# Attention and a cosine MLP on one core: global score products in tiles of 64 columns, and global value products two slots earlier

## The chip, the cores and the metric

The kernel runs on one core of a Trainium2 chip. The metric is the device time of one execution in microseconds (us). The kernel before takes 924.01 us, the median of three runs (923.69 to 924.47). Its profiled execution, from which all rows below are read, took 926.0 us with a span of 924.2 us.

A core has five engines that run side by side, each through its own list of instructions and in the order of that list: PE (TensorE, the matmuls; its weight loads are the extra line PEld), DVE (VectorE), ACT (ScalarE), POOL (GpSimd) and SP (SyncE, which starts most DMAs). They wait for each other only by semaphores. Matmuls write to PSUM, from which ACT and DVE read.

## The reference

```python
def _attn_ref(q_l, k_l, v_l, q_g, k_g, v_g):     # 8 batches, 8 heads, 512 local + 32 global rows, head size 64
    k_all = np.concatenate([k_g, k_l], axis=2)
    v_all = np.concatenate([v_g, v_l], axis=2)
    s_g = scale * np.matmul(q_g, k_all.transpose(0, 1, 3, 2))     # global rows see all 544 keys
    out_g = np.matmul(sm(s_g), v_all)
    ...                                           # s_ll: local rows see |i - j| <= 32, s_lg: and the 32 global keys
    out_l = np.matmul(sm(np.concatenate([s_lg, s_ll], axis=-1)), np.concatenate([v_g, v_l], axis=2))
    return np.concatenate([out_g, out_l], axis=2)

def _moe_ref(x, w_in, w_out):                     # x: 4608 x 512, w_in: 512 x 2048, w_out: 2048 x 512
    h = x @ w_in
    return ((h * np.cos(h)) @ w_out).astype(np.float32)
```

The rows of the attention's output, with the heads side by side, are the rows of `x`.

## The kernel before, in words

Every float32 number that goes into a product is split into a high and a low float16 part (names that end in h and l), and a product is the sum of three terms: high by high, low by high, high by low. For batches 0 to 2 the score products still run in float32.

**Attention.** A batch is cut into four units: two halves of the heads' groups by two halves of the rows. A unit multiplies queries and keys (`ps`, L574), takes the exponential (`t`, ACT), writes two planes of weights (`planes`), has them transposed by a DMA (`pt`, L704), and multiplies them with the values (`acc`, L746). ACT and DVE then split `acc` into `xh` (L769) and `xl` (L770), the inputs of the MLP. The global rows are a small side line of the same stages: scores `gps` (L789 in float32, L798 in float16) of four heads, minimum (`gt`, L811), exponential, planes `planes_g`, a transposing DMA to `ptg` (L839), value products `gacc` (L851), and a sum of these into `xg` on DVE (L866, L867), which is needed only for the last chunk of the MLP.

**MLP.** Chunks of 256 rows: `ph` = x by w_in (L923), eight of them in a chunk (`ph_0` to `ph_7`); ACT makes an integer of it (`u`, L946), DVE the rest (L947), ACT the cosine (`w`, L461), DVE the product (`gf`, L966), ACT its high part (`gh`, L970), POOL its low part (`gl`, L253), and PE multiplies with w_out (`po`, L996). `o` is the output on its way to memory.

**Order.** Work is put into slots: `at(slot, phase, f)` notes that the step f belongs to a slot and a phase of that slot. A unit has four slots, and its steps are placed relative to its own slot t: the scores of the global rows at `t + s_gs1`, the value products of the unit (`av_a`) at `t`, phase PA, the global value products (`g_f`) and their sum (`g_g`) at `t + s_gf`. From ranks made of slot and phase a list scheduler, which simulates the engines, writes the order of every engine's list. So a moved step also changes the order of steps that the diff does not touch.

**Buffers.** `gps`, `gacc`, `acc` and `ps` share PSUM tiles of the tag att (three buffers), `ph` has three, `po` two. `ptg` has one buffer.

**Start.** In the first 160 us the weights are still being split: `wo_hl` is written piece by piece (POOL, L253), and the first chunk's `po` products and some column sums of them (`po<-wo_hl,xh`) follow as the pieces come.

Of the kernel before, what the change touches and what calls it, by code (L numbers as in the profile page):

```python
# [23 lines left out]
SG = 32  # L24
# [80 lines left out]
FB = 3  # L105
# [10 lines left out]
s_gs1 = -4  # L116
s_gd = -3
s_ge = -1
s_gf = 2
s_v = -12  # L120
s_va = -8
W0 = -15
# [30 lines left out]
def body(tc, qf, v, wi, wo, mask, out):  # L153
    nc = tc.nc
    from contextlib import ExitStack

    with ExitStack() as ctx:
# [297 lines left out]
        st = {}  # L455
# [324 lines left out]
        def g_a(b, g, k):  # L780
            z, w = GW[k]
            pt = ps.tile([P, w], F32, tag="att", name=f"gps_{b}_{g}_{k}")

            for hh in range(4):
                if b >= FB:
                    break
                q, k_ = st["qk", b, k, 2 * g + hh // 2]
                c = hh % 2 * SG
                nc.tensor.matmul(  # L789
                    pt[32 * hh : 32 * hh + 32], q[:, c : c + SG], k_[:, z : z + w], start=True,  # L790
                    stop=True, tile_position=(0, 32 * hh), skip_group_check=True,
                )
            if b >= FB:
                for n, (x, y) in enumerate(((0, 2), (0, 3), (1, 2))):
                    for hh in range(4):
                        qk = st["qk", b, k, 2 * g + hh // 2]
                        c = hh % 2 * SG
                        nc.tensor.matmul(  # L798
                            pt[32 * hh : 32 * hh + 32], qk[x][:, c : c + SG], qk[y][:, z : z + w], start=n == 0,
                            stop=n == 2, tile_position=(0, 32 * hh), skip_group_check=True,  # L800
                        )
            st["gps", b, g, k] = pt

        def g_b(b, g, k):
# [230 lines left out]
        def at(slot, phase, f, *a, pr=None):  # L1035
            e = (phase, len(ev[slot]), f, a)
            ev[slot].append(e)
            pr = (slot, phase) if pr is None else pr if isinstance(pr, tuple) else (pr, phase)
            rank[slot, e[1]] = pr + (slot, e[1])
# [3 lines left out]
        def attn(b, h, g, o):  # L1043
            first = (b, h, g) < (0, 1, 0)
            if b or h and not EL:
                at(o["load"], PJ, load_qk, b, h, g)
            if b >= FB:
                at(o["load"] + s_qm - s_load, PG, q_m, b, h, g)
                at(o["host"], PC, q_s, b, h, g)
                at(max(o["host"], o["load"] + s_qh - s_load), PF, q_h, b, h, g)  # L1050
            for a in range(2):
                p = 2 * g + a
                at(o["sc"][a], PA, sc_a, b, h, p)
                for i in (2 * h, 2 * h + 1):
                    at(o["sc"][a], PA if first else PC, sc_b, b, p, i)
                    at(o["ex"][a], PI, sc_c, b, p, i)
                    at(o["sd"][a], PF, sc_d, b, p, i)
                    at(o["tr"][a], PA2, sc_e, b, p, i)
                if h == 0:
                    at(o["vd"][a], PF2, v_d, b, p, *((0,) if b == 0 else ()))  # L1060
                elif b == 0:
                    at(o["vd"][a], PF2, v_d, b, p, 1)
                at(o["av"][a], PA, av_a, b, h, p)
                at(-6 if first else o["av"][a], PF, av_b, b, h, p)
            at(o["gs"], PA, g_a, b, g, h)
            at(o["gs"], PA if first else PC, g_b, b, g, h)
            if h:
                at(o["ex"][1], PI, g_c, b, g)
                at(o["gd"], PF2, g_d, b, g)
                at(o["ge"], PA2, g_e, b, g)  # L1070
                at(o["gf"], PG, g_f, b, g)
                at(o["gf"], PH2, g_g, b, g)

        def steady(t):
# [23 lines left out]
        for g in range(2):  # L1098
            attn(0, 0, g, tight(U0 + 2 * g))
# [21 lines left out]
        for n in range(2, 4 * B):  # L1121
            b, h, g = n // 4, n // 2 % 2, n % 2
            t = 4 * n + T0 - EARLY.get(n, 0)
            if n % 4 == 0:
                at(t + s_v, PA0, load_v, b)
                at(t + s_va, PF, v_a, b)
                at(t + s_va, PG, v_b, b)
                at(t + s_va, PG2, v_c, b)
            attn(b, h, g, steady(t))
# [116 lines left out]
```

## Time and profile before

| what | value |
|---|---|
| median of three runs | 924.01 us |
| profiled execution, span | 926.0 us, 924.2 us |
| PE busy | 875.5 us, 95% of the span |
| ACT busy | 715.5 us, 77% |
| DVE busy | 635.9 us, 69% |
| POOL busy | 336.4 us, 36% |
| chain that ended last | PE 59%, ACT 17%, DVE 14% |

PE is busy nearly all the time, but its ends are modelled: a PE that waits a few tenths of a microsecond still reads as busy. Whether PE or ACT and DVE set the pace of a stretch is told by who waits for whom there. A row of a timeline gives the start, the duration, the engine, the line, the operation, output and inputs by their names, and in brackets how long the engine stood idle before it and who released it.

### The profile page before, as it was taken

The page shows a single profiled execution, that of the slowest core. Times are in us where ns is not written, and L with a number is a line of the kernel's source. Part 1 is how long each engine was busy: PE and PEld are TensorE (multiplying, and loading weights), DVE is VectorE, ACT ScalarE, POOL GpSimd, SP SyncE. Part 2 cuts the span into 40 slices and gives each one's busy share as a digit, 9 for nine tenths or more (in the row PEclk, how much of TensorE's full clock was granted, in tenths as well). Part 3 has the DMA queues.
Part 4 walks back from the last instruction along what each step waited for, and adds up shares of the span by engine and source line. Part 5 has one row for each costly group of instructions (what it writes and reads, how often), then busy time and mean ns, then how long its engine had stood idle before and what let it go on. Part 6 is the DMA issues. An engine that isn't in the chain of part 4 may idle for free.

```text
span 924.2 us, 21213 instructions
## 1 busy us (share of the span) xinstructions
PE 875.5 (95%) x8055; PEld 589.3 (64%) x8055; DVE 635.9 (69%) x1737; ACT 715.5 (77%) x1472; POOL 336.4 (36%) x690
## 2 busy tenths in 40 slices
PE   5568898999999999999999999999999999999998
PEld 3445564566666666666666666666666666666676
DVE  5997886367665967787768876796778766654221
ACT  6869987578777878888788878897888878865443
POOL 6838766233223222233223322332232322333232
PEclk9586998999999999999999999999999999999999
DMA  9949563344534435334534454444533332430000
GB/s 371 417 182 252 125 178 133 79 93 91 135 97 93 103 80 138 73 98 91 156 77 90 85 123 110 103 98 81 145 73 85 60 70 47 84 61 23 1 25 23
DMA packets 163943, 102.79 MB, mean 111 GB/s; under 512 B 149504, under 2 KB 149888, under 8 KB 161792
## 3 DMA queue, kind: packets, MB, share of 16 engines
q1 hardware_dynamic: 163840, 101.43, 43.7%
q8 instruction: 63, 1.03, 0.5%
q14 instruction: 40, 0.33, 0.1%
HBM read 55.79 MB, written 8.91 MB: 70 GB/s over the span
## 4 chain that ended last, share of the span: by engine, by line
PE 59%; ACT 17%; DVE 14%; issue 4%; POOL 3%; DMA 2%; SPq 0%; DVEq 0%; ACTq 0%; POOLq 0%
PE po L996 26%; PE ph L923 25%; ACT t L461 4%; PE ps L574 3%; ACT L461 3%; ACT w L461 3%; DVE u L947 2%; PE acc L746 2%; ACT planes L683 2%; DVE t L627 2%; DVE qkr L609 2%; ACT u L946 2%; ACT qh L608 1%; DMA raw_wi<-wi 1%; POOL wi_l L253 1%
## 5 line engine op out<-in xcount | busy, mean ns | idle before, releaser
L253 POOL TENSOR_TENSOR gl<-gf,gh 128x128 f16<-128x128 f32 x528 | 222.3, 452 | 443.5 <-ACT gh L970 423.6
L996 PE MATMUL po<-wo_hl,gh 128*128 128x512 f16 (+1 forms) x1088 | 314.3, 374 | 4.2 <-POOL wo_hl L253 4.1
L923 PE MATMUL ph<-xl,wi_h 128*128 128x256 f16 x1024 | 279.9, 274 | 1.7 <-DVE xl L770 1.7
L923 PE MATMUL ph<-xh,wi_h 128*128 128x256 f16 x1024 | 279.9, 275 | 0.6
L923 PE MATMUL ph<-xh,wi_l 128*128 128x256 f16 x1024 | 279.1, 274 | 0.0
L923 PEld LDWEIGHTS <-wi_h 128*128 128x128 f16 x2176 | 206.9, 98 | 48.3 <-issue 14.1
L996 PE MATMUL po<-wo_hl,gl 128*128 128x512 f16 (+1 forms) x544 | 199.8, 374 | 0.0
L996 PEld LDWEIGHTS <-gh 128*128 128x128 f16 x1088 | 106.6, 98 | 96.4 <-issue 1.6
L966 DVE SCALAR_TENSOR_TENSOR gf<-w,ph 128x512 f32<-128x512 f32 x136 | 93.3, 686 | 107.2 <-ACT w L461 107.0
L461 ACT ACTIVATE w<-u,pvs_hp,cs 128x512 f32<-128x512 f32 x136 | 110.3, 813 | 58.2 <-DVE u L947 56.5
L947 DVE SCALAR_TENSOR_TENSOR u<-u,cs,ph 128x512 f32<-128x512 int32 x136 | 101.3, 745 | 64.7 <-ACT u L946 64.6
L946 ACT ACTIVATE u<-ph,pvs_hp,cs 128x512 int32<-128x512 f32 x136 | 104.3, 768 | 28.5 <-PE ph L923 28.5
L461 ACT ACTIVATE t<-t,mn 128x192 f32<-128x192 f32 (+1 forms) x256 | 116.6, 458 | 6.1 <-DVE mn L627 5.8
L923 PEld LDWEIGHTS <-wi_l 128*128 128x128 f16 x1088 | 107.0, 98 | 18.1 <-issue 4.6
L970 ACT CAST gh<-gf 128x512 f16<-128x512 f32 x132 | 80.5, 610 | 38.5 <-DVE gf L966 30.3
L683 ACT ACTIVATE planes<-t,sm 128x224 f16<-128x224 f32 (+1 forms) x244 | 91.0, 453 | 5.2 <-DVE sm L650 5.2
L996 PEld LDWEIGHTS <-gl 128*128 128x128 f16 x544 | 53.4, 98 | 64.6 <-issue 5.3
L684 DVE SCALAR_TENSOR_TENSOR planes<-t,sm,planes 128x224 f16<-128x224 f32 (+1 forms) x244 | 92.4, 442 | 0.0
L461 ACT ACT_TABLE_LOAD x60 | 77.0, 1283 | 1.8 <-PEq L1236 0.7
L627 DVE CUSTOM_DVE_ANT_0 t<-ps,msk,qs 128x192 f32<-128x192 f32 (+1 forms) x160 | 59.7, 429 | 0.0
L769 ACT ACTIVATE xh<-acc,xs 128x256 f16<-128x256 f32 x64 | 29.4, 465 | 33.1 <-DVE xl L770 24.5
L746 PE MATMUL acc<-pt,vh 128*64 128x128 f16 (+2 forms) x896 | 45.8, 229 | 7.2 <-ACT pt L702 3.4
(187 smaller groups left out, 1099.3 us busy)
## 6 DMA issues: line engine op xcount, KB each, us to landing
qkr<-qf SPq DMA_DIRECT2D x32, 672.0 KB, 4.0
vr<-v SPq DMA_DIRECT2D x8, 1280.0 KB, 6.7
out<-o SPq DMA_DIRECT2D x33, 256.0 KB, 2.5
raw_wm<-wo SPq DMA_DIRECT2D x10, 512.0 KB, 11.3
raw_wi<-wi SPq DMA_DIRECT2D x4, 1024.0 KB, 16.8
wo_hl<-wi SPq DMA_DIRECT2D x4, 1024.0 KB, 19.0
raw_wo<-wo SPq DMA_DIRECT2D x8, 512.0 KB, 4.6
wi_h<-wo SPq DMA_DIRECT2D x4, 512.0 KB, 7.4
```

Of the source, the lines that this page charges most:

```text
L253: nc.gpsimd.tensor_tensor(o[..., c], a[..., c], b[..., c], op=op)
L461: ins = nc.scalar.activation(*a, **k).ins
L627: st["mn"] = nc.vector.tensor_tensor_reduce(t[:, h], pt[h], msk[:, MOFF[i] : MOFF[i] + w], nal, 3.0e38, ALU.add, ALU.min, mn[:, h : h + 1] ...
L683: a = nc.scalar.activation(hi, t[:, h], AF.Identity, scale=r)
L684: d = nc.vector.scalar_tensor_tensor(lo, t[:, h], r, hi, op0=ALU.mult, op1=ALU.subtract)
L746: mm = nc.tensor.matmul(acc[64 * h : 64 * h + 64, q_out : q_out + n0 * len(segs)], vt[:, tl, 64 * h : 64 * h + 64], rhs, start=(k == 0 and ...
L923: nc.tensor.matmul(ph[:, a], w[:, t // 8, kc, f], x[:, kc, q], start=first and ip == 0, stop=last and ip == 2, skip_group_check=True,)
L946: nc.scalar.activation(k, ph, AF.Identity, scale=st["cs", c][4], bias=quarter)
L947: nc.vector.scalar_tensor_tensor(u, k, m, ph, op0=ALU.mult, op1=ALU.subtract)
L966: nc.vector.scalar_tensor_tensor(gf, w, -0.5, st.pop(("ph", c, j)).rearrange("p a b -> p (a b)"), op0=ALU.mult, op1=ALU.mult,)
L970: nc.scalar.copy(gh, gf)
L996: mm = nc.tensor.matmul(po[n], g[:, a * CT + k * P : a * CT + (k + 1) * P], w[:, 2 * j + a, c0:c1], start=(j == 0 and i == 0), stop=(j == ...
```

## The change

Two things. First, a score tile `gps` holds four heads of 32 rows each. Before, each head has a matmul of its own, in a tile of 32 columns; now two heads that lie side by side in the same operand go in one matmul of 64 columns. There are two matmuls for a term in place of four. Second, `g_f` and `g_g` move from slot t+2 to slot t, and `g_f` from phase PG to phase PA2, behind the unit's own value products.

```diff
-s_gf = 2
+s_gf = 0
...
-            for hh in range(4):
-                if b >= FB:
-                    break
-                q, k_ = st["qk", b, k, 2 * g + hh // 2]
-                c = hh % 2 * SG
-                nc.tensor.matmul(
-                    pt[32 * hh : 32 * hh + 32], q[:, c : c + SG], k_[:, z : z + w], start=True,
-                    stop=True, tile_position=(0, 32 * hh), skip_group_check=True,
-                )
-            if b >= FB:
-                for n, (x, y) in enumerate(((0, 2), (0, 3), (1, 2))):
-                    for hh in range(4):
-                        qk = st["qk", b, k, 2 * g + hh // 2]
-                        c = hh % 2 * SG
-                        nc.tensor.matmul(
-                            pt[32 * hh : 32 * hh + 32], qk[x][:, c : c + SG], qk[y][:, z : z + w], start=n == 0,
-                            stop=n == 2, tile_position=(0, 32 * hh), skip_group_check=True,
-                        )
+            terms = ((0, 1),) if b < FB else ((0, 2), (0, 3), (1, 2))
+            for n, (x, y) in enumerate(terms):
+                for a in range(2):
+                    qk = st["qk", b, k, 2 * g + a]
+                    nc.tensor.matmul(
+                        pt[64 * a : 64 * a + 64], qk[x][:, : 2 * SG], qk[y][:, z : z + w], start=n == 0,
+                        stop=n == len(terms) - 1, skip_group_check=True,
+                    )
...
-                at(o["gf"], PG, g_f, b, g)
+                at(o["gf"], PA2, g_f, b, g)
                 at(o["gf"], PH2, g_g, b, g)
```

PE, at the end of batch 3's last local value products (`acc_1_2`; `gps_0_0` is a score tile of batch 4, `ph_0` the first product of the next chunk), before. A number behind the last underscore only tells tiles of a name apart:

```order
L746 MATMUL acc_1_2_6040<-pt_3_2_5959,vl_3_4809 64x128
L798 LDWEIGHTS qh_0_0_5561
L798 MATMUL gps_0_0_6077<-qh_0_0_5561 32x288
...
L798 MATMUL gps_0_0_6077<-qh_0_0_5561,qkr_0_0_5180 32x288
L923 LDWEIGHTS wi_h
L923 MATMUL ph_0_6116<-xh_4934,wi_h 128x256
```

The same place now:

```order
L746 MATMUL acc_1_2_5992<-pt_3_2_5911,vl_3_4779 64x128
L788 LDWEIGHTS qh_0_0_5519
L788 MATMUL gps_0_0_6029<-qh_0_0_5519 64x288
...
L788 MATMUL gps_0_0_6029<-qh_0_0_5519,qkr_0_0_5144 64x288
L841 LDWEIGHTS vh_2_4774
L841 MATMUL gacc_1_6036<-ptg_1_5914,vh_2_4774 64x2x32
...
L841 MATMUL gacc_1_6036<-ptg_1_5914,vl_3_4779 64x32
L913 LDWEIGHTS wi_h
L913 MATMUL ph_0_6105<-xh_4898,wi_h 128x256
```

The scores have half the matmuls, each of 64 columns as those of `acc` before them, and the 40 matmuls of `gacc`, which stood behind a later unit's `ps`, follow directly.

DVE at the same place, where it splits the two `acc` tiles, before:

```order
L609 SCALAR_TENSOR_TENSOR qkr_0_1_5564<-qkr_0_1_5564,qs_0_1_5971,qh_0_1_5976 128x1344
L770 SCALAR_TENSOR_TENSOR xl_4935<-acc_1_2_6040,xs,xh_4934 128x256
L811 ISA gt_0_6090,gmn_0_6091<-gps_0_0_6077,zero,qs_0_0_5556 128x288
L811 ISA gmn_0_6091 128x1
L770 SCALAR_TENSOR_TENSOR xl_4935<-acc_1_2_6040,xs,xh_4934 128x256
L966 SCALAR_TENSOR_TENSOR gf_7_6109<-w_7_6025,ph_7_5999 128x512
```

And now:

```order
L609 SCALAR_TENSOR_TENSOR qkr_0_1_5522<-qkr_0_1_5522,qs_0_1_5923,qh_0_1_5928 128x1344
L801 ISA gt_0_6077,gmn_0_6078<-gps_0_0_6029,zero,qs_0_0_5514 128x288
L801 ISA gmn_0_6078 128x1
L770 SCALAR_TENSOR_TENSOR xl_4899<-acc_1_2_5992,xs,xh_4898 128x256
L856 TENSOR_REDUCE xg<-gacc_1_6036 128x64
L549 SCALAR_TENSOR_TENSOR vl_3_6335<-vr_5197,vs_5675,vh_3_6334 128x640
L857 TENSOR_SCALAR xg<-xg,pvs_hp 128x64
L770 SCALAR_TENSOR_TENSOR xl_4899<-acc_1_2_5992,xs,xh_4898 128x256
L956 SCALAR_TENSOR_TENSOR gf_7_6098<-w_7_5977,ph_7_5951 128x512
```

The minimum `gt` now stands ahead of both `xl`, and `xg` with the value split `vl_3` of the next batch between them; before, these three stood some 13 us later.

PE in the start phase, first row of each stretch, before: `acc_0_0` is the first value product of batch 1, `po_0<-wo_hl,xh` waits for a piece of the weights:

```order
L746 MATMUL acc_0_0_1918<-pt_0_0_1728,vh_0_1433 64x128
...
L996 MATMUL po_0_1138<-wo_hl,xh_682 128x512
...
L746 MATMUL acc_0_0_1918<-pt_0_0_1728,vl_0_1434 64x128
...
L923 MATMUL ph_4_1998<-xh_680,wi_h 128x256
...
L923 MATMUL ph_5_2067<-xh_680,wi_h 128x256
...
L996 MATMUL po_0_1138<-wo_hl,xh_682 128x512
```

And now:

```order
L913 MATMUL ph_3_1865<-xh_676,wi_h 128x256
...
L746 MATMUL acc_0_0_1908<-pt_1_0_1833,vh_1_1429 64x64
...
L913 MATMUL ph_4_1986<-xh_676,wi_h 128x256
...
L913 MATMUL ph_5_2055<-xh_676,wi_h 128x256
...
L986 MATMUL po_0_1132<-wo_hl,xh_678 128x512
...
L913 MATMUL ph_5_2055<-xl_677,wi_h 128x256
```

All of `acc_0_0` (32 matmuls more), all of `ph_4` (24) and 7 of `ph_5` now stand ahead of the `po` group that stood behind the first 16 matmuls of `acc_0_0`.

## Rows read from the trace of the kernel before

**Rows 1.** Busy us (count) of PE, PEld, DVE, ACT, POOL in windows; PE clock, DMA
```profile
160.00:300.00 140.00, 139.95 (x1219) 91.67 (x1220) 85.24 (x245) 104.34 (x223) 42.97 (x95) 1.00 0.46 99
400.00:500.00 100.00, 99.51 (x979) 66.77 (x978) 76.62 (x210) 83.62 (x175) 29.66 (x67) 1.00 0.43 101
```

**Rows 2.** Waits from 160 to 300 us: total us, times, longest
```profile
ACT u L946 <- PE ph L923: 7.4, 6, 4.1
```

**Rows 3.** Waits from 300 to 800 us
```profile
ACT w L461 <- DVE u L947: 30.9, 35, 2.1
ACT xh L769 <- DVE xl L770: 21.5, 14, 1.7
...
PE ph L923 <- DVE xl L770: 1.7, 5, 0.4
```

**Rows 4.** Chain of waits, 440 to 492 us: start, us, what
```profile
443.46 0.76 PE gacc L851 x40
444.27 0.77 ACT u L946
...
487.73 2.56 PE ph L923 x22
```

**Rows 5.** Waits from 820 us to the end
```profile
ACT u L946 <- PE ph L923: 17.8, 14, 2.3
```

**Rows 6.** Timeline of PE around a score tile
```profile
332.28 0.28 PE L746 MATMUL acc<-pt,vh 128*64 128x128 f16 x4
332.39 0.22 PE L746 MATMUL acc<-pt,vl 128*64 128x128 f16 x2
332.54 0.31 PE L798 MATMUL gps<-qh 128*32 128x288 f16 x4
332.67 0.30 PE L798 MATMUL gps<-qkr,qh 128*32 128x288 f16 x4
```

**Rows 7.** Timeline of PE around the global value products
```profile
417.83 0.26 PE L574 MATMUL ps<-qkr,qh 64*128 64x224 f16 x2
417.92 0.26 PE L574 MATMUL ps<-qh,qkr 64*128 64x224 f16 x2
418.11 0.22 PE L851 MATMUL gacc<-ptg,vh 128*64 128x64 f16 x2
```

**Rows 8.** Timeline of SP: the transposing DMA of the global planes
```profile
421.50 1.30 SPq L839 DMA_TRANSPOSE ptg<-planes_g  x1
```

**Rows 9.** Timeline of DVE where two value tiles are split
```profile
435.96 0.51 DVE L811 CUSTOM_DVE_ANT_0 gt<-gps,zero,qs 128x288 f32<-128x288 f32 x1
436.58 0.48 DVE L770 SCALAR_TENSOR_TENSOR xl<-acc,xs,xh 128x256 f16<-128x256 f32 x1
438.79 0.69 DVE L966 SCALAR_TENSOR_TENSOR gf<-w,ph 128x512 f32<-128x512 f32 x1 [1.72 <-ACT w L461]
```

**Rows 10.** Timeline of ACT at that place
```profile
436.08 0.47 ACT L769 ACTIVATE xh<-acc,xs 128x256 f16<-128x256 f32 x1 [1.72 <-DVE xl L770]
```

**Rows 11.** Timeline of DVE at the old place of the sum
```profile
448.80 0.28 DVE L866 TENSOR_REDUCE xg<-gacc 128x64 f32<-128x128 f32 x1
449.00 1.07 DVE L549 SCALAR_TENSOR_TENSOR vl<-vr,vs,vh 128x640 f16<-128x640 f32 x1
449.99 0.41 DVE L867 TENSOR_SCALAR xg<-xg,pvs_hp 128x64 f32<-128x64 f32 x1
```

**Rows 12.** Timeline of ACT: two places where `w` waits for DVE
```profile
425.66 0.81 ACT L461 ACTIVATE w<-u,pvs_hp,cs 128x512 f32<-128x512 f32 x1 [1.53 <-DVE u L947]
...
451.10 0.81 ACT L461 ACTIVATE w<-u,pvs_hp,cs 128x512 f32<-128x512 f32 x1 [1.01 <-DVE u L947]
```

**Rows 13.** Start phase: timeline of PE and POOL, and a window
```profile
142.76 0.58 PE L996 MATMUL po<-wo_hl,xh 128*128 128x512 f16 x1 [4.59 <-POOL wo_hl L253]
...
154.46 1.30 POOL L253 TENSOR_TENSOR wo_hl<-z_wo,wo_hl 128x256 f16<-128x256 f32 x2 [1.09 <-DVE wo_hl L283]
...
140.40:147.30 6.90, 4.54 (x11) 1.57 (x11) 2.38 (x4) 4.20 (x12) 6.57 (x12) 0.51 0.36 137
```

## The prediction

> **What bounds the kernel now.** I read the windows first, then the waits inside them, then the chain. After the start phase PE is busy 139.95 of 140 us between 160 and 300 us and 99.51 of 100 in a later window, at full clock, while ACT has 83.62 and DVE 76.62 of 100 there [rows 1]. From the busy shares alone PE would set the pace all the way. The waits say something else, and I cut the run into four parts by them.
>
> From 160 to 300 us ACT waits for PE's products (7.4 us in 6 waits at `u`) [rows 2]: PE sets the pace. From 300 to 800 us ACT and DVE wait for each other (30.9 us at `w`, 21.5 us at `xh`), and it is PE that waits for DVE, 1.7 us in all at `ph`, for the split value tile [rows 3]. The chain of waits shows the same: PE holds it up to `gacc` at 443.46, ACT and DVE hold it from 444.27 on, and PE takes it back only at 487.73 [rows 4]. So once in a batch PE is caught by DVE, although it reads as 99.5% busy; its ends are modelled. In this part a shorter PE only waits longer, as long as ACT and DVE keep their pace. In the last part, from about 820 us, ACT waits for PE again, 17.8 us at `u` [rows 5]. The first, up to 160 us, is paced by the pieces of the weights: PE stands idle 4.59 us at 142.76 for POOL's `wo_hl`, and then runs at a granted clock of 0.51, the lower of its two levels [rows 13].
>
> A page of the Trainium skill goes against the busy share too: "Perfetto Trace Analysis", section Identifying the Most-Contended Engine, says that matmul busy time is no measure of headroom, that weight-load time is a better one, and that for ACT and DVE occupancy is a fair one. By it ACT (83.62) stands above PE's weight loads (66.77) in the middle part, and work taken off PE there is worth nothing; the trace agrees as far as the 1.7 us for which PE waits.
>
> **The change on PE.** A switch between shapes of matmuls costs time. The last `acc` pair starts at 332.39, the first score at 332.54; two `acc` pairs take 0.11 us (332.28 to 332.39), so one streams in 0.055, and 0.15 - 0.055 = about 0.096 is the switch [rows 6]. From `ps` to `gacc` it is 0.19 less the 0.09 between two `ps` rows, about 0.10 [rows 7]. In the new PE list `acc`, `gps` and `gacc` all write tiles of 64 columns and stand one behind the other. I count the neighbours in the lists: 47 switches fewer in all, 42 of them after 180 us (26 from `acc` to `gps`, 14 into `gacc`, 2 others; the way back into `ph` stays). Per batch in the middle that is 6, or 6 x 0.096 = 0.58 us.
>
> The stream of the scores itself costs nothing more or less: a term of four 32-column tiles takes 0.13 us [rows 6], which is one pass of 288 columns, since the four run side by side. Two tiles of 64 columns should do the same in one pass, since the pairs of `acc`, in just such tiles, also run side by side: x4 in the time of two passes [rows 6]. If the two ran one after the other, a term would take 0.26 (rival D). I take nothing. Bounds are 0 and +0.13 a term. The number of weight loads falls by 264; PEld is not the limit [rows 1].
>
> Is `ptg` there two slots earlier? Its transposing DMA is issued at 421.50 [rows 8], and the new place is behind the scores that `gt` reads at 435.96 [rows 9], some 10 us later. So PE gets no new wait; `ptg`, with its one buffer, is even freed sooner.
>
> **By parts of the run.**
>
> *160 to 300 us*, PE-paced: 8 switches gone by 0.096, -0.8 us.
>
> *300 to 820 us*, five batches, paced by ACT and DVE: here the new order on DVE counts, not the switches. At the end of a batch's second unit `gt` now stands before both `xl`, and `xg` and a `vl` stand between them. The `gt` adds 0.51 and a 0.08 read to what ACT's second `xh` waits for (it stands 1.72 us for that `xl` already) [rows 9, 10]: +0.56. The second `xl` comes 0.28 + 1.07 + 0.41 = 1.76 later [rows 11], less the 0.6 that `gt` had there, but ACT doesn't need it, and DVE has 1.72 us idle behind it before `gf` [rows 9], so I cost that at nothing; if that cover were gone it would be up to 1.2 a batch. PE will wait for it longer than now (about 1.5 in place of some 0.4), which it can afford since it no longer has the 0.76 of `gacc` at 443.46 [rows 4] ahead of it. What moves away is paid back where it stood: 1.76 us of DVE less in front of the `u` for which `w` waits 1.01 us at 451.10 [rows 11, 12]. Handed on, that is up to -1.76; I take -1.5, since `u` itself and the steps ahead of it keep their length. Two more places: in a batch's first unit `u` comes later behind the same three steps, and `w` at 425.66, which waits 1.53 us for it [rows 12], moves by +0.77 at most, by my working through the two lists with the rows' durations; in the next unit `gt` ahead of an `xl` (+0.5) and `gh` moved behind `u` (-0.5) cancel. Sum per batch: +0.56 - 1.5 + 0.77 + 0 = -0.2, five times -1.0. The bounds: without the pay-back +1.33 a batch, +6.7 in all; with the pay-back whole and no harm at 425.66, -1.2 a batch, and PE with its 0.58 less then stops it at about that, -3 in all.
>
> *From 820 us*, PE-paced: three switches, -0.3 us.
>
> *Up to 160 us*: in the new PE list 32 matmuls of `acc_0_0`, 24 of `ph_4` and 7 of `ph_5` stand ahead of the `po` group that waits 4.59 us [rows 13]. 31 `ph` by 2.56 / 22 = 0.116 us [rows 4] are 3.6 us, so the wait is nearly filled. It doesn't all come back, because the later groups wait for the later pieces: the last one is written at 154.46 + 1.30 = 155.76 [rows 13]. If the pieces stay where they are, the last group runs from about then, as it nearly does now, and what is gained is the work that stands ahead of it in the new list and behind it in the old: 5 of `ph_5` and 13 of `ph_6`, 18 x 0.116 = 2.1, and a set of `ps` of about 0.5: 2.6. I take -2.5. The bounds: the pieces may come earlier too, as their loads do in the lists of SP and POOL; then all of 4.59 and the lost half of the clock in the window from 140.4 to 147.3 (about 2) come back, -6.5. Or another step of the splitting comes late by one POOL row, 1.3 [rows 13], and the group order is worse: +2.
>
> **Sum:** -0.8 - 1.0 - 0.3 - 2.5 = -4.6. The profiled execution of 926.0 us would take 921.4; it lies 2.0 above the median of the runs, so I forecast 924.0 - 4.6 = 919.4 us.
>
> **Rivals.**
>
> A. *PE paces throughout.* Then all 42 switches after 180 us pay: -4.0, with the start -6.5: 917.5. For it: PE's 99.51 of 100. Against it: it waits for DVE [rows 3], and the chain passes to ACT and DVE.
>
> B. *The start gives nothing*, because the pieces and not PE's order set it: 924.0 - 2.1 = 921.9. For it: POOL's splits and their loads pace the stretch [rows 13]. Against it: behind the last piece PE has less left to do.
>
> C. *Slower:* the loop of ACT and DVE gets longer. If the DVE work that leaves the front of `u` at 450 is not on the way (because PE's later `ph` then sets `u`), and `gt` ahead of `xl` and the late `w` stay, +1.33 a batch is +6.7; with the other parts (-0.8 - 0.3 - 2.5) +3.1: 927.1. It decides from a pay-back under 0.6 us a batch. For it: PE waits 1.5 us at that `xl`, and its slack ahead of ACT afterwards is small. Against it: `w` waits for `u` and `u` for DVE in the rows of before, not for PE.
>
> D. *The wide score tiles don't run side by side.* 20 tiles of three terms by 0.13 add 7.8 us to PE, of which the waits and the saved switches take about half: 924 or so. Against it: the pairs of `acc`.
>
> **How the numbers follow.** The forecast 0.40, A 0.18, B 0.22, C 0.14, D 0.06. 0.2% is 1.85 us, about what a measurement of this kernel can tell from no change: faster is below 922.2, slower above 925.9. The forecast and A are faster; B lies at the edge, half of it and D are within; C is slower. With some of the forecast's tails: faster 0.66, within 0.20, slower 0.14. The range from 915.3 (A, with more from the start) to 925.5 leaves out most of C and the far end of A; the forecast's own is 917 to 922.
>
> **What would show it.** Right: the `acc` to score step near 0.055 instead of 0.15; `gacc` behind the scores without a wait; the 4.59 us wait of PE at `po` shrunk to about 1 and PE some 2.5 us ahead at 160 us; a batch as long as before or 0.2 shorter, with PE waiting longer at the second `xl` and `w` less at its place behind `u`. Wrong: ACT's `u` waiting for PE between 300 and 800 us, a batch that is longer, or a batch 0.5 us shorter, which is A.

## The result, and the profile after

The changed kernel takes 929.24 us (median of 4 runs, 928.61 to 930.77) against 923.85 of the kernel before beside it: a ratio of 1.006, interval 1.0042 to 1.0077. It is slower by 5.4 us; the forecast was 919.4 with a range up to 925.5. The profiled execution took 930.77 us, span 929.0. In the table of the experiments the ratios leave out runs in a slow state (2270 us in e1, 1787 in e6, 943 in one group of the kernel before) and the medians do not, which raises e1 by 0.2 us and e6 by 0.1.

The terms on PE came as forecast. Timeline of PE at the place of [rows 6, 7], after:

```profile
431.14 0.22 PE L746 MATMUL acc<-pt,vl 128*64 128x128 f16 x2
431.19 0.29 PE L788 MATMUL gps<-qh 128*64 128x288 f16 x2
431.31 0.29 PE L788 MATMUL gps<-qkr,qh 128*64 128x288 f16 x2
431.44 0.29 PE L788 MATMUL gps<-qh,qkr 128*64 128x288 f16 x2
431.56 0.20 PE L841 MATMUL gacc<-ptg,vh 128*64 128x64 f16 x2
```

From `acc` to the scores it is 0.05 us, one pair's stream, where it was 0.15; a term takes 0.12 (0.13 before), so the two wide tiles run side by side; `gacc` follows after 0.12 without a switch and without a wait for `ptg`. Yet PE is busy less, not because it is done sooner but because it waits. A window after (columns as in [rows 1]) and the waits from 300 to 800 us (total, times, longest, as in [rows 3]):

```profile
400.00:500.00 100.00, 97.39 (x940) 65.93 (x939) 75.90 (x208) 82.83 (x175) 29.18 (x66) 1.00 0.43 101
```

```profile
ACT w L461 <- DVE u L937: 26.9, 37, 1.8
PE ph L913 <- ACT xh L769: 8.3, 5, 2.0
PE ph L913 <- DVE xl L770: 2.6, 5, 0.6
```

PE's waits at `ph` grew from 1.7 us, all for `xl` [rows 3], to 8.3 for `xh` and 2.6 for `xl`. ACT is busy less too, 82.83 for 83.62 in the same 100 us: the loop of ACT and DVE got longer, with the same work in it. How much is read from `o` on ACT, which comes twice in a batch; these rows are the same one of the two in three batches running, first the kernel before, then after.

```profile
399.27 0.68 ACT L1014 ACTIVATE o<-po,cs 128x512 f32<-128x512 f32 x1
498.87 0.68 ACT L1014 ACTIVATE o<-po,cs 128x512 f32<-128x512 f32 x1
598.46 0.68 ACT L1014 ACTIVATE o<-po,cs 128x512 f32<-128x512 f32 x1
```

```profile
398.32 0.68 ACT L1004 ACTIVATE o<-po,cs 128x512 f32<-128x512 f32 x1
498.90 0.68 ACT L1004 ACTIVATE o<-po,cs 128x512 f32<-128x512 f32 x1
599.47 0.68 ACT L1004 ACTIVATE o<-po,cs 128x512 f32<-128x512 f32 x1
```

The changed kernel is 0.95 us ahead at 399 us, 0.03 behind at 499 and 1.01 behind at 598: **0.98 us a batch**, the same each time. At the end of the span it is 4.8 behind (929.0 against 924.2).

**Where in a batch.** The same difference of starts (after less before, the n-th `u` of ACT and the n-th `xl` and `qkr` of DVE in both profiles), from 407 us of before on: -0.94 at `u`, +1.16 at the `qkr` at 434, +1.60 at the `u` at 443, +0.11 at 457, +0.03 at 469. So the first unit gives away 2.10 us (forecast 0.77), the end of the second unit 0.44 (0.56), the old place of the sum pays back 1.49 (1.5), the next unit another 0.08. Three of the four terms were right. The first unit on ACT, after:

```profile
415.54 0.76 ACT L936 ACTIVATE u<-ph,pvs_hp,cs 128x512 int32<-128x512 f32 x1
416.20 2.26 ACT L548 ACTIVATE vh<-vr,vs 128x640 f16<-128x640 f32 x3
...
418.87 0.78 ACT L936 ACTIVATE u<-ph,pvs_hp,cs 128x512 int32<-128x512 f32 x1
419.54 0.81 ACT L461 ACTIVATE w<-u,pvs_hp,cs 128x512 f32<-128x512 f32 x1
422.04 0.81 ACT L461 ACTIVATE w<-u,pvs_hp,cs 128x512 f32<-128x512 f32 x1 [1.69 <-DVE u L937]
...
424.70 0.62 ACT L960 CAST gh<-gf 128x512 f16<-128x512 f32 x1 [1.34 <-POOL gl L253]
425.23 0.77 ACT L936 ACTIVATE u<-ph,pvs_hp,cs 128x512 int32<-128x512 f32 x1
426.82 0.81 ACT L461 ACTIVATE w<-u,pvs_hp,cs 128x512 f32<-128x512 f32 x1 [0.82 <-DVE u L937]
```

and DVE beside it, after:

```profile
421.27 0.73 DVE L937 SCALAR_TENSOR_TENSOR u<-u,cs,ph 128x512 f32<-128x512 int32 x1
...
423.94 0.68 DVE L956 SCALAR_TENSOR_TENSOR gf<-w,ph 128x512 f32<-128x512 f32 x1
426.03 0.75 DVE L937 SCALAR_TENSOR_TENSOR u<-u,cs,ph 128x512 f32<-128x512 int32 x1 [1.42 <-ACT u L936]
```

The numbers count the eight `ph` of a chunk from 0, so `u_4` to `u_6` are the fifth to the seventh. `u_4` now stands behind all eight planes and `u_5` behind three value splits, on both engines. Then `gh_5` starts only at 424.70, after a wait of 1.34 us, and `u_6`, right behind it in ACT's list, has to wait with it. The releaser that the row names, POOL's `gl`, isn't it: DVE's `gf_5` ends at 423.94 + 0.68 = 424.62, behind four `t`. `w_6` waited 1.53 us in [rows 12] and waits 0.82 now, but it comes at 426.82 against 425.66, from a head start of 0.94: 2.1 us lost.

The kernel before has the same two neighbours, `gh_5` and `u_6`, in the same order, but there `gh_5` doesn't wait. ACT at this place before, from `w_5` on, then DVE from `gf_5` on:

```profile
420.68 0.81 ACT L461 ACTIVATE w<-u,pvs_hp,cs 128x512 f32<-128x512 f32 x1
421.40 1.53 ACT L548 ACTIVATE vh<-vr,vs 128x640 f16<-128x640 f32 x2
422.84 0.60 ACT L970 CAST gh<-gf 128x512 f16<-128x512 f32 x1
423.35 0.77 ACT L946 ACTIVATE u<-ph,pvs_hp,cs 128x512 int32<-128x512 f32 x1
```

```profile
421.98 0.68 DVE L966 SCALAR_TENSOR_TENSOR gf<-w,ph 128x512 f32<-128x512 f32 x1
...
422.78 1.85 DVE L549 SCALAR_TENSOR_TENSOR vl<-vr,vs,vh 128x640 f16<-128x640 f32 x2
...
424.89 0.73 DVE L947 SCALAR_TENSOR_TENSOR u<-u,cs,ph 128x512 f32<-128x512 int32 x1
```

There `gf_5`, behind four `t` as well, ends at 422.66, two value splits keep ACT busy until `gh_5` at 422.84, and two splits and `xg` keep DVE busy until `u_6`. The new lists have these splits ahead of `u_5`: `gf_5` ends at 424.62, and nothing is left for ACT to do ahead of `gh_5`. What is new is therefore not the order of `gh_5` and `u_6` but the uncovered wait in front of them.

### The profile page after: what moved, and what is told of

Read it like the earlier page. It is cut to its first block, busy times and chain, and to the rows that moved or that the text cites. A ratio compares the mean times of both kernels' runs of the same rounds, so it can differ in the third digit from the quotient of the medians.

```text
span 929.0 us, 20863 instructions
## 1 busy us (share of the span) xinstructions
PE 871.9 (94%) x7887; PEld 592.4 (64%) x7887; DVE 638.3 (69%) x1737; ACT 716.9 (77%) x1472; POOL 334.3 (36%) x690
## 4 chain that ended last, share of the span: by engine, by line
PE 35%; ACT 22%; DVE 21%; issue 5%; DVEq 0%; ACTq 0%
PE po L986 17%; PE ph L913 15%; ACT t L461 5%; ACT L461 4%; ACT w L461 4%; DVE u L937 4%; DVE t L627 3%; DVE qkr L609 3%; ACT planes L683 3%; DVE gf L956 3%; DVE planes L684 2%; ACT qh L608 2%; ACT u L936 2%; DVE vm L512 1%; PE ps L574 1%
## 5 line engine op out<-in xcount | busy, mean ns | idle before, releaser
L253 POOL TENSOR_TENSOR gl<-gf,gh 128x128 f16<-128x128 f32 x528 | 220.0, 448 | 443.5 <-ACT gh L960 431.6
L684 DVE SCALAR_TENSOR_TENSOR planes<-t,sm,planes 128x224 f16<-128x224 f32 (+1 forms) x244 | 97.0, 461 | 0.1
L825 POOL TENSOR_TENSOR planes_g<-gt,planes_g 128x544 f16<-128x544 f32 x14 | 17.6, 1258 | 104.4 <-DVE planes_g L824 62.4
```

Of the source, the lines that this page charges most:

```text
L253: nc.gpsimd.tensor_tensor(o[..., c], a[..., c], b[..., c], op=op)
L684: d = nc.vector.scalar_tensor_tensor(lo, t[:, h], r, hi, op0=ALU.mult, op1=ALU.subtract)
```

## The experiments

Each median stands beside that of the kernel before, run on the same chip in turn; the interval is that of the ratio. Where a text says "order", `after(x, y)` puts x behind y in the list of their engine, without a wait. In the code batches count from 0, and `FB` is 3, the fourth. "A batch" is the change in the difference to the kernel before from one `o` to the next, as above.

| kernel | us | before | ratio, interval | a batch |
|---|---|---|---|---|
| changed kernel | 929.24 | 923.85 | 1.0042 to 1.0077 | +0.98 |
| e1 wide tiles alone | 927.82 | 924.41 | 1.0023 to 1.0049 | +0.35 |
| e2 move alone | 942.56 | 924.41 | 1.0179 to 1.0208 | +1.9 to +3.5 |
| e4 changed, old order of the first unit | 924.18 | 924.41 | 0.9989 to 1.0006 | -0.09 |
| e5 before, late u | 922.05 | 924.41 | 0.9961 to 0.9982 | -0.72 |
| e6 changed, gh behind u | 923.03 | 924.64 | 0.9971 to 0.9989 | -0.50 |
| e7 as e4, end of second unit | 931.95 | 924.64 | 1.0066 to 1.0091 | +0.6 to +2.7 |
| e8 changed, end of second unit | 940.25 | 924.64 | 1.0151 to 1.0186 | +2.9 to +4.6 |
| e9 from batch 4, both orders | 926.62 | 924.64 | 1.0016 to 1.0034 | +0.1 |
| e10 from batch 4 | 929.65 | 924.40 | 1.0044 to 1.0069 | +0.98 |
| e11 up to batch 3 | 925.60 | 924.40 | 1.0004 to 1.0022 | 0 from 500 us on |
| e12 changed, longer order | 923.98 | 924.40 | 0.9988 to 1.0006 | -0.27 |
| e13 from batch 4, move alone | 938.46 | 924.40 | 1.0137 to 1.0167 | +3.4 to +4.9 |
| e14 first batch, move alone | 928.12 | 924.25 | 1.0030 to 1.0055 | 0 |
| e15 first batch, wide tiles alone | 926.85 | 924.25 | 1.0015 to 1.0036 | 0 |
| e16 from batch 2, gh behind u | 922.04 | 924.25 | 0.9969 to 0.9987 | -0.52 |

**Which part, and is it the order? (e1, e2, e4, e5)**

e1, against the changed kernel:

```diff
-s_gf = 0
+s_gf = 2
-                at(o["gf"], PA2, g_f, b, g)
+                at(o["gf"], PG, g_f, b, g)
```

> The score tiles of 64 columns alone; the global value products and their sum stay in their old slots. Theory 1 (the 1.0 us that each batch of the changed kernel is longer comes from the order on ACT and DVE, above all from u of the fifth ph of the chunk behind all eight planes and three value splits ahead of the next u): this kernel has the order of before in the middle, so its batches keep their length and only the part paced by PE gains, 6 x 0.096: 922.5 to 924 us. Rival 2 (PE's longer wait at the second xl sets the pace): the same, the gacc is in its old place. Rival 3 (two tiles of 64 columns don't run side by side): 928 us or more, and a term of the scores at 0.25 us.

e2, against the kernel before:

```diff
-s_gf = 2
+s_gf = 0
-                at(o["gf"], PG, g_f, b, g)
+                at(o["gf"], PA2, g_f, b, g)
```

> The move of the global value products and their sum alone; score tiles of 32 columns. Theories 1 and 2: the loss is all here, 929 to 931 us, a batch 1.0 us longer in the middle. Rival 3: 922 to 924 us.

e4, against the changed kernel:

```diff
+        def weights(b, p, i, h, a, d):        # a, d: planes on ACT and DVE
+            if b >= FB and p >= 2 and i >= 2 and (p, i, h) > (2, 2, 0):
+                after(a, st["uA", 2 * b, 4])
+                after(d, st["uD", 2 * b, 4])
+        def values(b, p, x, y):               # x, y: vh on ACT, vl on DVE
+            if b > FB and p in (1, 2):
+                after(x, st["wA", 2 * b - 2, 5])
+                after(y, st["uD", 2 * b - 2, 5])
```

> The changed kernel with four orders (without waits) added in each batch from the fourth on: all planes but the first behind u of the fifth ph on ACT and DVE, and two of the value splits behind w and u of the sixth, as before. gacc, gt and xg stay where the change put them. Theory 1: the first unit of a batch no longer gives away 2.1 us, the pay-back of 1.5 us at the old place of xg stays, so a batch is shorter than before by what PE allows, some 0.6 us: 919 to 922 us. Rival 2: PE still waits about 2.4 us at the second xl and the batch stays 1.0 us longer: 928 to 929.5 us.

e5, against the kernel before:

```diff
+        def weights(b, p, i, h, a, d):
+            if FB <= b < B and p >= 2 and i >= 2:
+                after(st["uA", 2 * b, 4], a)
+                after(st["uD", 2 * b, 4], d)
+        def values(b, p, x, y):
+            if b > FB and p in (1, 2):
+                after(st["uA", 2 * b - 2, 5], x)
+                after(st["uD", 2 * b - 2, 5], y)
+                if p == 2:
+                    after(st["wA", 2 * b - 2, 4], st["uA", 2 * b - 2, 5])
```

> The kernel before with the opposite orders in each batch from the fourth on: u of the fifth ph behind all eight planes on ACT and DVE, u of the sixth behind three value splits, w of the fifth behind u of the sixth. The global products stay in their old slots. Theory 1: 2.1 us are given away in each of four to five first units and nothing is paid back: 931 to 934 us. Rival 2: 923 to 925 us, since PE meets the same xl as before.

Neither part alone did what was expected: e1 lost 3.3 us (by its ratio), e2 18. In e1 a batch is 0.35 us longer; there too `gt` stands ahead of both `xl`, and ACT's second `xh` loses 0.43. The rest of its 3.3 is put down to the start (e15 below), by what is left over. e4 takes 5 us off the changed kernel and makes its batch as long as before, even 0.09 shorter, which is near the forecast of -0.2; its first unit gives away 1.03 us in place of 2.10. That spoke for theory 1. e5 refuted its first form: `u_4` comes 2.5 us later than in the kernel before, and the batch is 0.72 us *shorter*. ACT in e5:

```profile
415.06 0.76 ACT L963 ACTIVATE u<-ph,pvs_hp,cs 128x512 int32<-128x512 f32 x1
...
420.32 0.78 ACT L963 ACTIVATE u<-ph,pvs_hp,cs 128x512 int32<-128x512 f32 x1 [0.20 <-PE ph L940]
421.74 0.81 ACT L461 ACTIVATE w<-u,pvs_hp,cs 128x512 f32<-128x512 f32 x1 [0.64 <-DVE u L964]
422.46 0.60 ACT L987 CAST gh<-gf 128x512 f16<-128x512 f32 x1
423.00 0.81 ACT L461 ACTIVATE w<-u,pvs_hp,cs 128x512 f32<-128x512 f32 x1
```

Here `u_6` (420.32) stands ahead of `w_5` and of `gh_4`, and `gh_5` comes far behind, so nothing that waits for `gf_5` is in front of it; `w_6` runs at 423.00 in place of 425.66 [rows 12]. A late `u` does no harm by itself. The second theory: what costs is that `u_6` stands behind `gh_5` and its wait.

**Which wait? (e6, e7, e8, e9)**

e6, against the changed kernel:

```diff
+        def tail(c, j):                       # called behind gh of chunk c, j
+            if c >= 2 * FB and c % 2 == 0 and c < NC and j == 6:
+                for k in (4, 5):
+                    after(st["ghA", c, k], st["uA", c, 6])
```

> The changed kernel with one pair of orders in each batch from the fourth on: gh of the fifth and sixth ph behind u of the seventh on ACT, two places later. Nothing else is moved; u of the fifth stays behind the eight planes. Theory 1 as it stands now (a late u costs nothing by itself; what costs 1.3 to 1.5 us a batch is that u of the seventh stands behind gh of the sixth, which waits 1.3 us for a gf that DVE has behind four t): a batch gets 1.3 to 1.5 us shorter than in the changed kernel until PE stops it, 922 to 924.5 us. Theory 1 in its first form (the late u itself): less than 0.3 us a batch, 927.5 to 929.5. Rival 2 (PE's wait at the second xl): 929.

Two `gh` in each batch stand behind one `u` in place of in front of it, and 6.2 us are gone (7.0 when each is taken against its own kernel before). The lists of PE and POOL are those of the changed kernel, instruction by instruction, and DVE's differs in one place near 733 us, so this is the cleanest of the experiments. ACT in e6:

```profile
421.06 0.81 ACT L461 ACTIVATE w<-u,pvs_hp,cs 128x512 f32<-128x512 f32 x1 [1.69 <-DVE u L964]
421.78 0.76 ACT L963 ACTIVATE u<-ph,pvs_hp,cs 128x512 int32<-128x512 f32 x1
422.44 0.60 ACT L987 CAST gh<-gf 128x512 f16<-128x512 f32 x1
423.72 0.62 ACT L987 CAST gh<-gf 128x512 f16<-128x512 f32 x1 [0.68 <-DVE gf L983]
424.33 0.81 ACT L461 ACTIVATE w<-u,pvs_hp,cs 128x512 f32<-128x512 f32 x1
```

`w_5` still waits its 1.69 us, but `u_6` runs at once, `gh_5` still waits, 0.68 us, but behind `u_6`, and `w_6` comes without a wait at 424.33, 2.49 earlier than in the changed kernel, whose profile is 0.98 later before this place: 1.5 us a batch, as expected. PE still waits at the second `xl`, 2.8 us in 5 waits as against 2.6, so rival 2 falls.

e8, against the changed kernel (e7 has the same beside the lines of e4, e9 beside those of e6 and with the change from the fourth batch on only):

```diff
+        def total(b, g):
+            if FB <= b < B - 1 and g == 1:
+                after(st["gt", b + 1, 0, 0], st["last_x", b, 1, 2][1])
+                after(st["gt", b + 1, 0, 0], st["last_x", b, 1, 3][1])
+                after(st["xg", b, 1], st["last_x", b, 1, 3][1])
+        def values(b, p, x, y):
+            if b > FB and p == 3:
+                after(x, st["last_x", b - 1, 1, 3][0])
+                after(y, st["last_x", b - 1, 1, 3][1])
```

> The kernel with the early u and late value splits (924.2 us) and in addition, at the end of each batch's second unit, gt, xg and the value split behind both xl, and vh behind both xh. If the 0.44 us that gt costs in front of xl is all that is left there: 0.4 us a batch less, 922 to 923. If PE's wait at the second xl sets the pace (rival 2): more than that, 920 to 921. If the moved steps come late for u later on: 924 or more.

> The changed kernel with the orders at the end of the second unit alone (gt, xg and the value split behind both xl). Rival 2 (PE's waits of 1.8 and 0.6 us there set the pace): the waits go and a batch is 1 us or more shorter, 924 to 925. Theory 1: 0.44 us a batch at most, 927 to 928.

> Both parts of the change from the fourth batch on only, so that everything before 330 us is the list of before, with gh behind u as in the first of this group and with gt, xg and the value split behind both xl. Theory 1 as it stands now: a batch 0.6 us shorter than before, as far as PE allows, with no change in the start: 921 to 922.5 us. Rival 2: 920 to 922. If neither place is what costs: 928 to 930.

e8 and e9 missed, and e7 is in its open last branch ("924 or more") but not for the reason given there: with `xl` ahead, e7 and e8 lost 8 and 11 us against their bases, e4 and the changed kernel (7.5 and 10, each against its own kernel before). PE in e8, and its clock there (last three columns: clock, DMA, GB/s):

```profile
434.88 0.27 PE L946 MATMUL ph<-xh,wi_h 128*128 128x256 f16 x1 [1.81 <-ACT xh L800]
436.57 0.37 PE L946 MATMUL ph<-xl,wi_h 128*128 128x256 f16 x1 [1.42 <-DVE xl L801]
...
437.59 1.06 PE L1020 MATMUL po<-wo_hl,gh 128*128 128x512 f16 x2
```

```profile
434.00:442.00 8.00, 5.70 (x27) 3.09 (x27) 5.88 (x14) 6.25 (x14) 0.00 (x0) 0.79 0.02 8
```

The scheduler placed PE's work anew as well: the `po` that stood between the two waits in the changed kernel stand behind them. Two waits in a row, 3.2 us with one matmul between, and the granted clock is at its lower level for a while behind them (0.79 in the mean of 8 us; two `po` take 1.06 for 0.59). Then ACT's `u` waits for PE: 1.15 us at 450.46. So these two runs don't measure what they were made for, the 0.44 us of `gt`. They show a cliff near the changed kernel, whose profile falls off it in one batch only:

```profile
736.00:744.00 8.00, 6.11 (x30) 3.36 (x30) 6.24 (x14) 6.53 (x12) 0.00 (x0) 0.79 0.01 2
```

From 400 to 700 us its clock is 1.00 throughout. From 700 us to the end the difference grows by 2.8 us instead of 0.98, and this is part of it. What tips it is open: in that batch PE waits 2.0 us for `xh` and 0.4 for `xl`, and the profile of e10 (below) has 2.0 and 0.6 at the same place with the clock at 1.00 throughout. In e9 the clock holds, and a batch still is 0.1 us longer, not 0.6 shorter. The 0.44 of `gt` is gone there: the difference to the kernel before is +0.42 at the `qkr` ahead of it and +0.42 at ACT's second `xh` (+1.16 and +1.60 in the changed kernel). But `vh`, which in the changed kernel sits between the two `xh` where ACT waits anyway, now costs 0.7 us behind them (+1.14 at the next `u`).

**Start or middle? (e10, e11, e12, e13)**

e10, and the mirror e11 (`b >= FB` for `b < FB`), each with the score tiles of 64 columns in the same batches:

```diff
-                at(o["gf"], PA2, g_f, b, g)
-                at(o["gf"], PH2, g_g, b, g)
+                w = 2 * (b < FB)
+                at(o["gf"] + w, PG if w else PA2, g_f, b, g)
+                at(o["gf"] + w, PH2, g_g, b, g)
```

> Both parts of the change from the fourth batch on only: every engine's list is that of before up to there and as in the changed kernel after it. If the loss is all in the middle (the profiles give +5.7 us from 300 us to the end): 929.5 to 930.5 us. If the start of the changed kernel loses too: 927 to 929. If PE's switches had paid in the middle as in rival A: 921.

> The mirror of the kernel before this: both parts of the change in the first three batches only, the old order from the fourth on. The forecast's terms (-2.5 in the start, -0.8 in the part paced by PE): 921 us. By what the changed kernel leaves when +5.7 is taken off its +5.4: 923.5 to 924.5 us, the start giving nothing.

The middle and the end alone cost 5.25 us (e10). The first three batches alone cost 1.2 (interval 0.4 to 2.0) where the forecast had -3.3. The part paced by PE did its -0.8: in e11's profile the difference goes from -1.01 at 197 us to -1.79 at 306. Behind that, where its lists go over to those of before, it loses 1.0 again (-0.75 at the end). So the start loses about 1 us (1.2 + 0.8 - 1.0, give or take the 0.8 of the interval) instead of winning 2.5. The changed kernel against e10 says nearly the same: 5.4 and 5.25 us, so the first three batches gain nothing in it.

e12, against the changed kernel:

```diff
+        def values(b, p, x, y):
+            if b > FB and p == 1:
+                after(y, st["tD", b, 0, 1])
+        def tail(c, j):
+            if c >= 2 * FB and c % 2 == 0 and c < NC and j == 6:
+                after(st["ghA", c, 4], st["uA", c, 6])
+                after(st["wA", c, 5], st["uA", c, 6])
+                after(st["ghA", c, 5], st["wA", c, 6])
+                after(st["gfD", c, 5], st["uD", c, 6])
```

> The changed kernel with a longer set of orders in the first unit of each batch from the fourth on, after the pattern of the kernel that beat the one before: u of the seventh ph ahead of w of the sixth and of both gh, the sixth gh behind w of the seventh, and two value splits behind the four t on DVE. Theory 1 as it stands: at least as fast as the swap of gh and u alone (923.0), 919.5 to 922.5, with PE as the next limit. If the swap had already taken all of it: 922.5 to 923.5.

It missed both ranges and gave nothing beyond e6 (-0.27 a batch against -0.50; the medians stand 0.95 apart). ACT's `u` now waits for PE, 5.0 us in 4 waits from 300 to 800 us (none in e6), which speaks for PE as the next limit but doesn't show it.

e13, the lines of e10 put into the kernel before (with `s_gf = 0`), so the move from the fourth batch on with tiles of 32 columns:

> The move of the global value products from the fourth batch on only, with score tiles of 32 columns: the lists of before up to there. Compared with the kernel that has both parts there. If the wide tiles only save switches: 0.4 us a batch more than with both, 931 to 933 us. If without that saving PE comes late behind the second xl, so that ACT's u waits for it and TensorE's clock falls there: 2 to 3 us a batch more, 935 to 938 us.

938.46, the worse of the two. Its difference grows by 3.4 to 4.9 us a batch, ACT's `u` waits for PE, and the clock falls:

```profile
ACT u L946 <- PE ph L923: 10.7, 8, 1.8
```

```profile
436.00:444.00 8.00, 8.00 (x42) 4.45 (x41) 5.01 (x13) 5.61 (x13) 1.58 (x4) 0.70 0.94 245
```

This is rival C as the prediction told it (PE's later `ph` sets `u`), with the clock on top. Its first unit gives away 2.1 us too. In the changed kernel, and in e10, which differs from e13 in the wide tiles and the lists that follow from them, this hardly comes up: from 300 to 800 us ACT's `u` waits once for PE in the changed kernel, 0.5 us, and not in e10.

**The start (e14, e15, e16)**

e14 is e13's edit with `(b > 0)`, the move in the first batch alone; e15 has the wide tiles in the first batch alone; e16 is e6 with both parts of the change from the second batch on:

> The kernel before with the move of the global value products in the first batch alone (32-column tiles); every list is that of before again from about 180 us on. The forecast for the start was -2.5 us with both parts; the two parts in the first three batches together measured +1.2 us, of which -0.8 is the part paced by PE, so the start loses about 2. If the early place of the global value products makes PE wait there (for ptg, 2.5 us in the changed kernel's profile): 926 to 927. If the wide tiles' other order does it: 924 to 925.

> The kernel before with the 64-column score tiles in the first batch alone; from about 180 us on every list is that of before. If the wide tiles' other order of the start costs: 926 to 927. If the move costs: 924 to 925.

> Both parts of the change from the second batch on, with gh behind u as in the kernel that took 923.0 us; the first batch keeps its lists. If the start is what the 923.0 still loses, about 2 us: 920.5 to 921.5. If it is not: 922.5 to 923.5.

Each part alone costs there, 3.9 and 2.6 us, more than the two together in the first three batches (1.2 in e11). Waits of PE from 60 to 165 us, first before, then after:

```profile
PE po L996 <- POOL wo_hl L253: 8.7, 4, 4.6
PE pm_wo L217 <- DVE d_wo L209: 8.7, 1, 8.7
```

```profile
PE pm_wo L217 <- DVE d_wo L209: 10.1, 1, 10.1
PE ph L913 <- DVE gf L956: 3.0, 3, 2.0
PE gacc L841 <- DMA ptg<-planes_g: 2.5, 1, 2.5
PE pm_v L490 <- DVE d_v L484: 2.3, 1, 2.3
PE acc L746 <- DMA pt<-planes: 1.7, 4, 0.7
PE acc L746 <- DVE wo_hl L283: 1.4, 1, 1.4
PE po L986 <- POOL wo_hl L253: 0.8, 1, 0.8
```

The 8.7 us of waiting for weights went down to 0.8, as forecast, and 12 us of other waits stand earlier: `pm_wo` 1.4 longer, then `gf`, the transposed planes `ptg`, and the rest. The wait for `ptg` is not in e14, which was made for it: there PE waits 5.0 us for `pt` and 5.1 for `wo_hl`. So which wait costs in the start stays open. e16, which leaves the first batch as it was, takes 922.04 against e6's 923.03, between its two ranges; against their own kernels before the ratios are 0.9978 and 0.9980, so it doesn't show that anything comes back. e5, e6 and e16 beat both kernels.

## Why the prediction was wrong

**The step that failed most** is the one on a batch's first unit, "`w` at 425.66 ... moves by +0.77 at most, by my working through the two lists". It moved by 2.1. I had followed `u`, the value splits and `w`, and not `gh_5`, which stands in front of `u_6` on ACT in both kernels. The value splits that moved ahead of `u_5` had covered its wait; with them ahead `gf_5` ends 2 us later on DVE, and `gh_5` and `u_6` wait 1.34 us for it. The working put that wait at nothing. e6 takes `u_6` out from behind it and gets 1.5 us a batch, and with the change a batch is then 0.5 us shorter than before. The +0.77 is near what is left: e6 gives away 0.59 in the first unit (-1.92 before it, -1.33 behind it). The 2.10 and the 0.44 less the pay-back of 1.49 and the 0.08 of the next unit make the +0.98 a batch; the change from the fourth batch on alone costs 5.25 us (e10).

**The second is the start**, -2.5. That the wait for `wo_hl` would be filled was right; that its time would come back was not: the start loses about 1 us. The term counted PE's order around one wait, and not that every list of the first 140 us is another one, on which PE waits elsewhere (12 us of waits in the changed kernel's profile). "So PE gets no new wait" for `ptg` was right for the middle and wrong for the first batch, 2.5 us in that profile.

**What held:** the switches (0.096 each, 0.8 us in the part paced by PE), the wide tiles side by side, so not rival D; the 0.44 for `gt` ahead of `xl`, forecast 0.56 (gone in e9); the pay-back of 1.49, forecast 1.5; that the switches in the middle pay nothing, so not rival A. PE's longer wait came, but at the second `xh` (1.8 us) and not at the second `xl` (0.6), where the prediction had 1.5. By the rule cited for this (the Trainium skill, "Perfetto Trace Analysis", Identifying the Most-Contended Engine) ACT has the larger share in the middle, and the measurement agrees that PE's saved time is not what a batch is made of; but ACT's 82.83 of 100 doesn't show the limit either, which is a loop of waits between two engines.

**Rival C** came near in time (927.1) and sign, with another mechanism in the changed kernel: the pay-back came in full, and the loss was in the first unit. Its own mechanism is part of what makes e2 and e13 so slow. The last part, forecast -0.3, is +0.64 in the profile (+4.13 to +4.77 from 806 us on); why stays open.

## What to carry to other kernels

A change that moves one step makes a list scheduler rewrite the lists of all engines: read the new lists instruction by instruction where two engines wait for each other, and for each one ask what stands in front of it, what that one waits for, and what work covers that wait, not only what it needs itself. A `gh` in front of an `u` cost nothing while two value splits covered its wait, and 1.5 us a batch when they had moved away, more than all switches saved there (0.58). And where a stretch is full of tuned orders and loads, as a start, don't book a filled wait as a gain: here other waits took its place.

## What the runs showed of the hardware

The switch from `acc`'s tiles of 64 columns to score tiles of 32 cost TensorE about 0.096 us, that from `ps` to `gacc` about 0.10, and none is seen between `acc`, `gps` and `gacc` when all three write 64 columns (0.05 and 0.12 us from one to the next, the stream alone). Behind two waits of PE of 1.8 and 1.4 us with one matmul between, the granted clock stood at its lower level for some microseconds (e8, 0.79 in the mean of 8 us). With 1.5 us of `po` between them, waits of 1.8 and 0.6 left it at 1.00 in three batches of the changed kernel; in the next one, with 2.0 and 0.4, it fell, and with 2.0 and 0.6 in e10 it did not, so the lengths of the waits alone don't tell. And two executions with the same lists up to 330 us stood 2.2 us (e10) and 3.4 us (e13) ahead of the profile of the kernel before at 300 us: the start of a single profile says nothing about a change of that size, only the timed runs do.
